# The last q/k group through a staging tile and small DMAs, with a new order of all operations

## The chip, the cores and the metric

The kernel runs on one core of a Trainium2 chip. The metric is the device time of that core in microseconds. Three runs of the kernel before took 193.17, 193.51 and 193.54 us; the median is 193.51. Texts below call the engines TensorE (PE in the profile; its weight loads PEld), VectorE (DVE), ScalarE (ACT), GpSimd (POOL) and SyncE (SP), which issues all DMAs here.

## The reference

The input x has 2048 rows of 448 numbers in bf16. Two layers are applied, each with a residual:

```python
h  = x + A(layernorm(x))          # qkv (448 x 1344), 16 heads of 28 channels,
                                  # 8 keys at distances 0, 2, .. 14 back, softmax, * wo
h2 = h + B(h):
  g  = gelu(layernorm(h) @ w1)    # 448 x 448
  hs = [g0 shifted +1, g1 shifted -1, g2 shifted +2, g3 shifted -2] @ w2   # four groups of 112 channels
  x1 = h + hs
  B  = x1 + gelu(layernorm(x1) @ w3) @ w4     # 448 x 1792, 1792 x 448
```

In the attention every query row reads only its own key and the seven keys 2, 4, .. 14 rows back. So a block of rows needs the last keys of the block before it.

## The kernel before, in words

**Stages.** The 2048 rows are handled in four steps t = 0..3 of 512 rows. For each the program has these phases; the digit behind a name is its t. N1 is the first normalization and A1 the transposes of x and the q and k channels (TensorE sums, copied out of PSUM, the banks where sums are made). V is the value channels. A2 is the products of queries and shifted keys on VectorE (four per step, c = 0..3, into `qk_r`), which TensorE adds up. S is the softmax, with the product `pb` (weights times reciprocal sum) and copies `pt` of its transposes. A3 builds band matrices on VectorE (`bd_r`, four per step), which TensorE multiplies with the values `vw`; copies `actT` bring the result out. O is the product with wo and the residual in `xin`. B1 is the next normalization with a DMA transpose, M the product with w1 and its gelu. Then the rows go through five units u = 0..4 of 2, 4, 4, 4 and 2 tiles of 128 rows: B2 (product with w2, residual), T (normalization and a DMA transpose), W3 (product with w3, gelu into `h3T`) and B3 (product with w4, last residual, and the store to the output). "A23" is phase A2 of step 3, "T0" phase T of unit 0, and so on.

**The last q/k group.** In A1 three pairs of groups hold 128 channels of q and of k each. The last 64 channels of q and of k stand in one pair of PSUM banks X and Y: X for the first 256 of the 512 rows, Y for the other 256, with q in partitions 0 to 63 and k in 64 to 127. q must go to `qT` (two halves of 64 partitions side by side), k to `kr`, which holds four runs of 64 keys on each of two halves of the partitions, and ahead of each run the PADK = 16 keys before it (the shared keys, or halo). Each step copies them with 8 operations (6 for t = 3): per bank one copy of q (64x256) and one of k (64x256), then a halo of 64x64, one of 64x48, and for t < 3 one of 64x16 into the next step's `kr` and one of 128x48 from `kk[t]` to `kk[t+1]`, the other keys' halo. These are 30 operations in all, of ScalarE but for one.

**What sets the order.** All operations are recorded with numbers by `S.add` and `S.group`. `arrange` puts them into the sequence that the list ORDER gives, which holds all numbers; every engine, and SyncE's queue of DMAs too, runs its own operations in that order. So an operation that waits holds back everything that stands behind it on its engine. Waits on semaphores follow from which data an operation reads and writes and from the buffers of the pools (`_Pool`): an operation that takes a buffer waits for all that used it last. The list OTHER names operations that go to their alternative engine: copies out of PSUM and norms have such an alternative, and the softmax product `pb` has GpSimd as its own (two of four are in OTHER). The strings NORM, STATS, POWER and the like choose engines of parts of the normalizations per step. All instructions are emitted at one line, L987, so in the profile names and shapes tell them apart, not lines. L982 loads a table of ScalarE's functions.

The copies in question:

```python
for h, b in enumerate((X, Y)):
    copy(qT[64 * h:64 * h + 64, 3, now:now + 256], b(lambda v: v[0:64, 0:256]))
    copy(kr[t][64 * h:64 * h + 64, :, PADK:], b(...v[64:128, 0:256]...), False)
copy(kr[t][64:128, :, 0:PADK], last(X, 0, 4), False)
copy(kr[t][0:64, 1:4, 0:PADK], last(Y, 0, 3), False)
```

The program's DMAs are loads (x in six pieces, then wqkv, wo, w1, w2, w3, w4), the copies of `vt` to `vw` (four per step, three for t = 0: vwa, vwb, vwc and vwp), one DMA transpose for each B1 and T, and the stores. The loads stand early in SyncE's order, the w4 loads among those of the attention.

Of the kernel before, what the change touches and what calls it, by code (L numbers as in the profile page):

```python
# [5 lines left out]
ACT = mybir.ActivationFunctionType  # L6
# [11 lines left out]
RESIDUAL = 'ttvv'  # L18
ORDER = """
# [30 lines left out]
"""  # L50
OTHER = """
104 127 196 197 199 402 408 411 519 525 528 582 583
# [79 lines left out]
class _Sched:  # L132
# [59 lines left out]
    def arrange(self, sequence, other=()):  # L192
# [4 lines left out]
        done = set()  # L197
        self.gorder = []
        for n, k in enumerate(sequence):
# [3 lines left out]
            op.deps |= op.sdeps  # L203
            for d in op.deps | op.odeps:
                if d not in done:
                    raise RuntimeError("operation %d (%s) stands before %d (%s)" % (k, op.tag, d.idx, d.tag))
# [68 lines left out]
def bass_sequential_preLN__sliding_local_dilated__mixer_s_mlp__prompt_kernel(  # L275
# [25 lines left out]
    A_W4 = A_W + 4 * (1344 + 128)  # L301
    A_QG = A_W4 + NF * 448
# [6 lines left out]
    with ExitStack() as es:  # L309
# [17 lines left out]
        st6 = sb("st6", [128, 8, 6], F32)  # L327
        mv = sb("mv", [128, 3, NTL, 2], F32)
# [20 lines left out]
        P_h3 = _Pool("h3", lambda k: h3T[:, k, :], NF + 2)  # L349
        P_st = _Pool("st", lambda k: st6[:, k, :], 8)  # L350
# [70 lines left out]
        def load_x(i, n):  # L421
            return dma("x%d" % i, xin[:, i:i + n, :], xv[:, i:i + n, :], 128 * n * D * 2)

        def load_rows(chan, dst, src, lo, n):

            for h in range(2):
                dma("%s%s" % (chan, "ab"[h]), dst[:, 2 * h:2 * h + 2, :], src[192 * h:192 * h + 256, lo:lo + n].rearrange("(c k) n -> k c n", k=128), 256 * n * 2)
# [21 lines left out]
        w4_v = B_w4.rearrange("(f k) n -> k f n", k=128)  # L449
        for f in range(0, NF, 7):  # L450
            dma("w4%d" % f, w4_s[:, f:f + 7, :], w4_v[:, f:f + 7, :], 128 * 7 * D * 2)
        for eng in ("sp", "pool", "act"):
            loads = [op for op in S.ops if op.tag == "load" and op.eng == eng]
            for a, b in zip(loads, loads[1:]):
                b.odeps.add(a)
# [164 lines left out]
        def setup_late(after):  # L620
# [18 lines left out]
            late("memset", ap=vw[0:PADK, 0, 0, :], constant=0.0)  # L639
            late("memset", ap=gT[:, :, 0:2], constant=0.0)  # L640
# [31 lines left out]
        def phase_A1(t):  # L672
# [356 lines left out]
```

## Time and profile before

| What | Value |
|---|---|
| median of three runs | 193.51 us (193.17 to 193.54) |
| the profiled execution: time, span | 193.18 us, 191.7 us |
| granted TensorE clock, mean | 0.999 |
| TensorE busy | 181.3 us, 95% of the span, 2482 matmuls |
| VectorE busy | 129.5 us, 68% |
| ScalarE busy | 132.9 us, 69% |
| GpSimd busy | 29.3 us, 15% |
| DMA, moved in all | 17.03 MB |
| chain that ended last | 66% TensorE, 21% ScalarE, 5% VectorE, 2% DMA |

The span is the time from the first to the last instruction of one profiled execution; the run's own time lies 1.5 us above it. Busy times are sums over an engine's instructions. The rows of the groups name what is written and what is read (`out<-in`), the shape, the count, the busy time, the mean of one in ns, and the idle time of the engine just ahead of them. The chain of waits goes back from the last instruction to what released each; in a timeline each row is a run of like instructions with start and duration.

### The profile page before, as it was taken

Reading aid. Unit: us, or ns where it says so; the run is one execution under the profiler, and the core shown is the slowest. Engines: PE = TensorE matmul, PEld = TensorE weight load, DVE = VectorE, ACT = ScalarE, POOL = GpSimd, SP = SyncE. Lnnn points to the kernel's source line nnn. Section 1 sums busy time; section 2 is a strip of 40 time slices with the busy share of each in tenths; the row PEclk is TensorE's granted clock in tenths of the full one; section 3 lists DMA queues with packets and bytes.
Section 4 is the critical chain, followed back from the end, with each engine's and each line's share of the span. In section 5 each row is a group of like instructions: output and inputs, shape, how many; then the busy total and the mean of one; then the engine's idle time right before and its main releaser. Section 6 shows DMA issues by size and latency. Waiting matters only on the chain.

```text
span 191.7 us, 5740 instructions
## 1 busy us (share of the span) xinstructions
PE 181.3 (95%) x2482; PEld 92.6 (48%) x2482; DVE 129.5 (68%) x229; ACT 132.9 (69%) x310; POOL 29.3 (15%) x63
## 2 busy tenths in 40 slices
PE   6999999999999868989999999999999999999994
PEld 2584533453444333347545444455444544555672
DVE  7799999999999999899876960036988022002203
ACT  4579999999999999999594998860148004821340
POOL 3240000000004000202076000022077600000000
PEclk9999999999999999999999999999999999999999
DMA  5999791004604179480805024006100812000111
GB/s 144 349 268 186 190 320 36 10 3 118 149 3 85 28 64 262 140 178 5 109 3 113 2 50 87 0 3 146 36 27 0 164 51 72 0 3 0 51 48 48
DMA packets 30272, 17.03 MB, mean 89 GB/s; under 512 B 18936, under 2 KB 29736, under 8 KB 30248
## 3 DMA queue, kind: packets, MB, share of 16 engines
q1 hardware_dynamic: 30248, 16.68, 36.7%
q8 instruction: 19, 0.31, 0.7%
q14 instruction: 5, 0.04, 0.1%
HBM read 8.04 MB, written 1.84 MB: 51 GB/s over the span
## 4 chain that ended last, share of the span: by engine, by line
PE 66%; ACT 21%; DVE 5%; DMA 2%; POOL 1%; issue 1%; SPq 1%; POOLq 0%; ACTq 0%
PE ps L987 66%; ACT arena L987 7%; ACT lntm L987 4%; ACT actT L987 2%; DMA vw<-vt 2%; ACT vt L987 2%; ACT L982 1%; DVE lntm L987 1%; DVE st L987 1%; SPq L987 1%; ACT xin L987 1%; ACT ls L987 1%; ACT L987 1%; DVE bd_r L987 1%; DVE actT L987 1%
## 5 line engine op out<-in xcount | busy, mean ns | idle before, releaser
L987 PE MATMUL ps<-actT,arena 64*128 64x256 bf16 (+1 forms) x756 | 68.8, 329 | 1.3 <-DVE arena L987 0.7
L987 ACT ACTIVATE h3T<-ps 128x512 bf16<-128x512 f32 (+1 forms) x70 | 30.3, 525 | 39.3 <-PE ps L987 39.2
L987 PEld LDWEIGHTS ps<-actT,arena 64*128 64x128 bf16 x756 | 35.5, 94 | 30.7 <-PE ps L987 2.1
L987 PE MATMUL ps<-arena,h3T 64*128 64x448 bf16 (+2 forms) x434 | 44.4, 344 | 0.0
L987 ACT ACTIVATE arena<-ps 128x512 bf16<-128x512 f32 (+10 forms) x86 | 40.1, 515 | 3.5 <-PE ps L987 2.8
L987 DVE SCALAR_TENSOR_TENSOR ost<-ps,mrs,arena 128x448 bf16<-128x448 f32 (+1 forms) x17 | 10.6, 652 | 36.4 <-PE ps L987 36.4
L987 DVE TENSOR_TENSOR qk_r<-arena 128x4096 bf16<-128x4096 bf16 (+1 forms) x16 | 32.0, 2017 | 0.7 <-PE ps L987 0.5
L987 PEld LDWEIGHTS ps<-arena,h3T 64*128 64x128 bf16 (+1 forms) x434 | 23.0, 94 | 18.7 <-issue 0.2
L987 POOL TENSOR_TENSOR arena<-arena,xin 128x448 f32<-128x448 f32 x16 | 17.2, 1091 | 45.3 <-DVE lntm L987 45.3
L987 DVE TENSOR_TENSOR bd_r<-arena,bmask 80x2048 bf16<-80x2048 bf16 x16 | 18.9, 1213 | 0.9 <-PE ps L987 0.7
L987 ACT ACTIVATE actT<-ps 128x512 bf16<-128x512 f32 (+2 forms) x21 | 14.6, 743 | 2.1 <-PE ps L987 2.1
L987 PE MATMUL ps<-wo_s,actT 64*128 64x448 bf16 x128 | 14.3, 351 | 0.6 <-DVE actT L987 0.4
L987 PE MATMUL ps<-actT,w_s 64*128 64x512 bf16 x112 | 13.3, 377 | 1.5 <-ACT rs_y L987 0.7
L987 PE MATMUL ps<-arena,actT 64*128 64x448 bf16 x112 | 12.4, 350 | 0.4 <-ACT vt L987 0.4
L987 PE MATMUL ps<-w_s,arena 64*128 64x448 bf16 x112 | 11.6, 350 | 0.9 <-ACT arena L987 0.7
L987 ACT ACTIVATE lntm<-xin,nm 128x448 bf16<-128x448 bf16 x16 | 10.5, 661 | 2.6 <-DVE nm L987 2.6
L987 DVE SCALAR_TENSOR_TENSOR arena<-xin,rs_y,ps 128x448 f32<-128x448 bf16 x16 | 10.3, 672 | 2.1 <-PE ps L987 2.0
L987 DVE TENSOR_SCALAR lntm<-arena,mv,rs_y 128x512 bf16<-128x512 f32 x14 | 10.2, 774 | 2.1 <-POOL rs_y L987 2.0
L987 POOL TENSOR_TENSOR pb<-ls,mx 128x512 bf16<-128x512 f32 x2 | 3.3, 1640 | 52.6 <-ACT mx L987 52.6
L987 DVE BATCH_NORM_STATS2 st<-xin 128x6 f32<-128x448 bf16 x16 | 9.4, 614 | 0.8 <-DMA xin<-in_A_x_dram 0.8
L987 PEld LDWEIGHTS ps<-actT,w_s 64*128 64x128 bf16 x112 | 5.2, 94 | 8.6 <-PE ps L987 1.7
L987 PEld LDWEIGHTS ps<-wo_s,actT 64*128 64x128 bf16 x128 | 5.6, 94 | 7.2 <-PE ps L987 1.4
(73 smaller groups left out, 161.9 us busy)
## 6 DMA issues: line engine op xcount, KB each, us to landing
arena<-in_B_w_dram SPq DMA_DIRECT2D x2, 896.0 KB, 6.7
out_dram<-ost SPq DMA_DIRECT2D x15, 112.0 KB, 1.8
arena<-in_B_w_dram SPq DMA_DIRECT2D x2, 784.0 KB, 5.7
vw<-vt SPq DMA_DIRECT2D x4, 320.0 KB, 4.3
vw<-vt SPq DMA_DIRECT2D x4, 256.0 KB, 4.3
arena<-in_A_wqkv_dram SPq DMA_DIRECT2D x2, 448.0 KB, 5.0
xin<-in_A_x_dram SPq DMA_DIRECT2D x2, 448.0 KB, 7.5
xin<-in_A_x_dram SPq DMA_DIRECT2D x3, 224.0 KB, 5.6
```

The costliest lines, as they stand in the source:

```text
L982: eng.preload_act_table_set("natural_log_exp_and_others")
L987: inst = getattr(eng, meth)(**kw)
```

## The change

Each bank of the last q/k group is copied whole (128x256) into a staging tile `stg`, of which there is one buffer. From there DMAs put the parts in place: two for q (`sq`), two for k (`sk`), and the halos by `kra`, `krb`, and for t < 3 `krc` and `kkc`. The 30 copies become 8 copies (of ScalarE, as the new OTHER has none of them) and 30 DMAs of 2 to 32 KB on SyncE.

Beside it:

- ORDER and OTHER are new. By the new OTHER, all four copies of A32, one more norm of B10 and one of T1 are on ScalarE (two of these copies and both norms were on VectorE); the other way go one copy 128x1024 of A12, one more copy of A10, one `vt` copy of V3 and one `pt` copy of S3. Of A33's four copies two are on VectorE as before, but not the same two.
- `pb` has no alternative any more: all four are on VectorE, where two were on GpSimd.
- NORM for unit 1 lets ScalarE do its norms, with VectorE as the alternative (three of four take it), which adds two small operations (`nm`, `nmr`) on VectorE.
- The tile for w4 lies over that of wqkv, and the w4 loads stand behind V3 (`load_w4`).
- Output staging has five buffers instead of three.
- The weight loads of wo, w1, w2 and w3 stand later in SyncE's order, among the small DMAs. krb3 stands right behind T0's DMA transpose, and two of V3's `vw` DMAs behind B12's.
- COPIED and ALONE are empty and false, and the code under them does nothing; more general slices in some sums change no instruction.

Operations go from 891 to 901, DMAs on SyncE from 71 to 101, ScalarE's operations from 272 to 251, VectorE's from 219 to 222, GpSimd's from 59 to 57. TensorE has the same matmuls.

```diff
-NORM = {'N0': 'vvvv', 'N1': 'avvv', 'B1': 'avvv', 'B2': 'avvvv'}
+NORM = {'N0': 'vvvv', 'N1': 'vvvv', 'B1': 'avvv', 'B2': 'aavvv'}
-NBD, NLN, NACT, NSM, NO = 3, 2, 4, 1, 3
+NBD, NLN, NACT, NSM, NO = 3, 2, 4, 1, 5
+HALO = 'dddd'
+STAGE = 'dddd'
 ORDER = """
...
 OTHER = """
-104 127 196 197 199 402 408 411 519 525 528 582 583
+99 104 196 199 355 502 529 533 539 590 591 652 653 654
...
-    A_W4 = A_W + 4 * (1344 + 128)
-    A_QG = A_W4 + NF * 448
+    A_W4 = A_W
+    A_QG = A_W4 + max(NF * 448, 4 * (1344 + 128))
...
+        P_sg = _Pool("sg", lambda k: stg[:, k, :, :], 1)
...
             duo(half(X, 0, True), half(Y, 64, False), ((0, 256),))
-            for h, b in enumerate((X, Y)):
-                copy(qT[64 * h:64 * h + 64, 3, now:now + 256], b(lambda v: v[0:64, 0:256]))
-                copy(kr[t][64 * h:64 * h + 64, :, PADK:], b(lambda v: v[64:128, 0:256].rearrange("p (j n) -> p j n", j=4)), False)
-            copy(kr[t][64:128, :, 0:PADK], last(X, 0, 4), False)
-            copy(kr[t][0:64, 1:4, 0:PADK], last(Y, 0, 3), False)
-            if t + 1 < NST:
-                copy(kr[t + 1][0:64, 0:1, 0:PADK], last(Y, 3, 1), False)
-                copy(kk[t + 1][:, :, 0:PADK], kk[t][:, :, 512:KVW])
+            if STAGE[t] == "d":
+                stage = _Tile(P_sg)
+                for h, b in enumerate((X, Y)):
+                    copy(stage(lambda v, h=h: v[:, h, :]), b(lambda v: v[:, 0:256]))
+                for h in range(2):
+                    dma("sq%d%d" % (t, h), qT[64 * h:64 * h + 64, 3, now:now + 256], stage(lambda v, h=h: v[0:64, h, :]), 64 * 512)
+                    dma("sk%d%d" % (t, h), kr[t][64 * h:64 * h + 64, :, PADK:], stage(lambda v, h=h: v[64:128, h, :].rearrange("p (j n) -> p j n", j=4)), 64 * 512)
...
+            if HALO[t] == "d":
+                if STAGE[t] == "d":
+                    end = lambda h, lo, n: stage(lambda v: v[64:128, h, :].rearrange("p (j n) -> p j n", j=4)[:, lo:lo + n, 64 - PADK:])
...
+                dma("kra%d" % t, kr[t][64:128, :, 0:PADK], end(0, 0, 4), 64 * 4 * PADK * 2)
+                dma("krb%d" % t, kr[t][0:64, 1:4, 0:PADK], end(1, 0, 3), 64 * 3 * PADK * 2)
+                if t + 1 < NST:
+                    dma("krc%d" % t, kr[t + 1][0:64, 0:1, 0:PADK], end(1, 3, 1), 64 * PADK * 2)
+                    dma("kkc%d" % t, kk[t + 1][:, :, 0:PADK], kk[t][:, :, 512:KVW], 128 * 3 * PADK * 2)
...
-            S.add("dve", "tensor_tensor", alts=[("pool", [("tensor_tensor", mult)])], **mult)
+            dve("tensor_tensor", **mult)
...
+        def load_w4():
+            last = S.ops[-1]
+            w4_v = B_w4.rearrange("(f k) n -> k f n", k=128)
+            for f in range(0, NF, 7):
+                dma("w4%d" % f, w4_s[:, f:f + 7, :], w4_v[:, f:f + 7, :], 128 * 7 * D * 2).odeps.add(last)
```

More of the change, by code (lines that the diff above doesn't have):

```diff
@@ L203, in arrange @@
             op.deps |= op.sdeps
+            if not ALONE:
+                pass
+            elif op.insts[0][0] == "dma_start_transpose":
+                op.deps.update(turned + moved)
+                turned, moved = [op], []
+            elif op.is_dma and not callable(op.chan):
+                op.deps.update(turned)
+                moved.append(op)
             for d in op.deps | op.odeps:
@@ L327, in bass_sequential_preLN__sliding_local_dilated__mixer_s_mlp__prompt_kernel @@
         st6 = sb("st6", [128, 8, 6], F32)
+        stg = sb("stg", [128, 1, 2, 256], BF16)
+        gM = sb("gM", [128, max(1, len(COPIED)), QGW], BF16) if COPIED else None
         mv = sb("mv", [128, 3, NTL, 2], F32)
@@ L448, in bass_sequential_preLN__sliding_local_dilated__mixer_s_mlp__prompt_kernel @@
         load_rows("w3", w3_s, B_w3, 0, F)
[L449 to L455, printed above, removed]
+        loads = [op for op in S.ops if op.is_dma]
+        for a, b in zip(loads, loads[1:]):
+            b.odeps.add(a)
         TOP, BOT = slice(0, 64), slice(64, 128)
@@ L639, in setup_late @@
             late("memset", ap=vw[0:PADK, 0, 0, :], constant=0.0)
+            if COPIED:
+                late("memset", ap=gM[64:128, :, 0:2], constant=0.0)
+                late("memset", ap=gM[64:128, :, 2 + SEQ:4 + SEQ], constant=0.0)
             late("memset", ap=gT[:, :, 0:2], constant=0.0)
@@ new lines, in phase_A1 @@
+            if HALO[t] == "d":
+                if STAGE[t] == "d":
+                    end = lambda h, lo, n: stage(lambda v: v[64:128, h, :].rearrange("p (j n) -> p j n", j=4)[:, lo:lo + n, 64 - PADK:])
+                else:
+                    end = lambda h, lo, n: kr[t][64 * h:64 * h + 64, lo:lo + n, 64:]
+                dma("kra%d" % t, kr[t][64:128, :, 0:PADK], end(0, 0, 4), 64 * 4 * PADK * 2)
[3 more added lines that the diff above has]
+                    dma("kkc%d" % t, kk[t + 1][:, :, 0:PADK], kk[t][:, :, 512:KVW], 128 * 3 * PADK * 2)
+            else:
+                copy(kr[t][64:128, :, 0:PADK], last(X, 0, 4), False)
+                copy(kr[t][0:64, 1:4, 0:PADK], last(Y, 0, 3), False)
+                if t + 1 < NST:
+                    copy(kr[t + 1][0:64, 0:1, 0:PADK], last(Y, 3, 1), False)
+                    copy(kk[t + 1][:, :, 0:PADK], kk[t][:, :, 512:KVW])
@@ L847, in evict @@
                         lo, m, early = MOVED[g]
-                        at = 2 + t * 512 - early
+                        now = 2 + t * 512
+                        at = now - early
                         skip = max(0, -at)
-                        act(gT[lo:lo + m, g, at + skip:at + 512], b(lambda v: v[lo:lo + m, skip:]), ACT.Gelu_apprx_tanh)
+                        to = gM if g in COPIED else gT
+                        if g in COPIED:
+                            dma("gm%d%d" % (t, g), gM[lo:lo + m, g, at + skip:at + 512], gT[lo:lo + m, g, now + skip:now + 512], m * 1024)
+                            rest = slice(64, lo) if lo > 64 else slice(lo + m, 128)
+                            dma("gn%d%d" % (t, g), gM[rest, g, now:now + 512], gT[rest, g, now:now + 512], (64 - m) * 1024)
+                        else:
+                            act(gT[lo:lo + m, g, at + skip:at + 512], b(lambda v: v[lo:lo + m, skip:]), ACT.Gelu_apprx_tanh)
                         if t == NST - 1:
-                            dve("memset", ap=gT[lo:lo + m, g, at + 512:at + 512 + early], constant=0.0)
-                return sums(lambda lo, n: b(halves(lambda v: v)), lambda c, part: w1_s[part, c, g * 128:(g + 1) * 128],
-                            lambda c, part, lo, n: rows(a, c, 0, 4, part), upper), evict
+                            dve("memset", ap=to[lo:lo + m, g, at + 512:at + 512 + early], constant=0.0)
+                return sums(lambda lo, n: b(halves(lambda v: v[:, lo:lo + n], n // 128)), lambda c, part: w1_s[part, c, g * 128:(g + 1) * 128],
+                            lambda c, part, lo, n: rows(a, c, lo // 128, n // 128, part), upper), evict
             for g in (0, 2):
@@ L874, in side @@
                     part = (TOP, BOT)[h]
-                    return [(gT[part, c, 2 + i * 128 + SHIFT[c, h]:130 + i * 128 + SHIFT[c, h]], (lambda lo, m, c=c: w2_s[part, c, lo:lo + m])) for c in range(n)]
+                    return [((gM if h and c in COPIED else gT)[part, c, 2 + i * 128 + SHIFT[c, h]:130 + i * 128 + SHIFT[c, h]], (lambda lo, m, c=c: w2_s[part, c, lo:lo + m])) for c in range(n)]
                 def out():
@@ L910, in group @@
                 b = _Tile(P_bank)
-                return sums(lambda lo, m: b(halves(lambda v: v[:, 0:128 * n], n)), lambda c, part: w3_s[part, c, f * 128:(f + 1) * 128],
-                            lambda c, part, lo, m: rows(a, c, 0, n, part), upper), \
+                return sums(lambda lo, m: b(halves(lambda v: v[:, lo:lo + m], m // 128)), lambda c, part: w3_s[part, c, f * 128:(f + 1) * 128],
+                            lambda c, part, lo, m: rows(a, c, lo // 128, m // 128, part), upper), \
                     lambda: act(h3[u][f](lambda v: v[:, 0:128 * n]), b(lambda v: v[:, 0:128 * n]), ACT.Gelu_apprx_tanh)
```

22 lines of the change are left out of this document (16 added, 6 removed), and 60 rows, old and new, of the table ORDER.

## The prediction

> **What bounds the kernel now.** I read the busy time by stage first, because the page's 95% for TensorE is a mean over stages with different limits. The columns are the stretch in us, its length, and busy time and count of each engine.
>
> ```profile
> 60.00:76.00 16.00, 12.69 (x250) 5.86 (x248) 15.76 (x25) 15.60 (x36) 2.20 (x1) 1.00 0.63 116
> 76.00:88.00 12.00, 11.02 (x132) 5.11 (x130) 11.13 (x26) 11.71 (x26) 2.56 (x4) 1.00 0.55 148
> 88.00:104.00 16.00, 15.53 (x300) 8.67 (x302) 12.50 (x25) 12.72 (x29) 5.97 (x7) 1.00 0.35 53
> 104.00:188.00 84.00, 84.00 (x871) 43.92 (x868) 32.05 (x71) 39.30 (x81) 13.30 (x15) 1.00 0.19 45
> ```
>
> From 104 to 188 us TensorE (first count) is busy all the time and the other two less than half of it, so nothing done to VectorE or ScalarE there can shorten it. From 60 to 88 us VectorE and ScalarE are both full, and TensorE is idle for 3.31 + 0.98 = 4.3 us; from 88 to 104 us for another 0.47 us. The granted clock is 1.00 throughout. So the kernel ends earlier only if TensorE idles less ahead of about 100 us: there are 4.8 us to be had in these stretches, and lighter work on one of two full engines brings them only if the other gets no heavier.
>
> The chain of waits says where the last stretch without a gap begins:
>
> ```profile
> 100.41 87.81 PE ps L987 x907
> ```
>
> Hence I look for the event that releases this stretch. It is an `actT` copy on VectorE, which the two timelines about that moment show (start, duration, engine, operation; in brackets the idle time ahead and its releaser):
>
> ```profile
> 94.58 1.22 DVE L987 TENSOR_TENSOR bd_r<-arena,bmask 80x2048 bf16<-80x2048 bf16 x1 [0.70 <-PE ps L987]
> 95.72 0.68 DVE L987 CAST actT<-ps 128x512 bf16<-128x512 f32 x1
> 96.33 0.23 DVE L987 BATCH_NORM_AGGREGATE mv<-st 128x2 f32<-128x6 f32 x2
> 96.59 0.17 DVE L987 TENSOR_SCALAR rs_x<-mv 128x4 f32<-128x4 f32 x1
> 97.90 1.86 DVE L987 TENSOR_SCALAR lntm<-arena,mv,rs_y 128x512 bf16<-128x512 f32 x2 [1.14 <-POOL rs_y L987]
> 99.68 0.68 DVE L987 CAST actT<-ps 128x512 bf16<-128x512 f32 x1
> ```
> ```profile
> 98.14 0.42 PE L987 MATMUL ps<-bd_r,vw 80*32 80x64 bf16 x32
> 98.49 1.50 PE L987 MATMUL ps<-arena,h3T 64*128 64x448 bf16 x14
> 100.41 0.93 PE L987 MATMUL ps<-wo_s,actT 64*128 64x448 bf16 x8 [0.43 <-DVE actT L987]
> ```
>
> The last band product of attention (94.58) ends at 95.80; the TensorE batch that reads it starts 2.34 us later, so that wait had room. The copy that O3 (·wo of the last 512 rows) needs stands behind two of T1's norms, which waited 1.14 us for GpSimd's power: TensorE lost 0.43 us there.
>
> **The change on ScalarE.** All 30 small copies of the last q/k group leave the engines; eight copies 128x256 from PSUM come instead. The groups by shape (busy us, mean ns):
>
> ```profile
> L987 ACT ACTIVATE h3T<-ps 128x256 bf16<-128x256 f32 x28 | 8.6, 406 | 11.1 <-PE ps L987 11.0
> ...
> L987 ACT ACTIVATE actT<-ps 128x512 bf16<-128x512 f32 x12 | 6.8, 615 | 2.1 <-PE ps L987 2.1
> L987 ACT ACTIVATE actT<-ps 128x1024 bf16<-128x1024 bf16 x6 | 6.2, 1077 | 0.0
> L987 ACT ACTIVATE arena<-ps 64x256 bf16<-64x256 f32 x15 | 5.6, 376 | 2.3 <-PE ps L987 2.1
> ...
> L987 ACT ACTIVATE arena<-ps 64x64 bf16<-64x64 f32 x4 | 0.9, 216 | 0.1
> L987 ACT ACTIVATE arena<-arena 128x48 bf16<-128x48 bf16 x3 | 0.8, 268 | 0.0
> L987 ACT ACTIVATION_READ_ACCUMULATOR xin<-ps 128x1 f32 x4 | 0.8, 201 | 0.0
> L987 ACT ACTIVATE lntm<-xin,nmr,rs_y 128x512 bf16<-128x512 bf16 x1 | 0.8, 803 | 0.0
> ```
>
> Out: 5.6 + 0.9 + 0.8 = 7.3 us, and four copies 64x48 and three 64x16, each at no more than the 0.216 of the 64x64 row, 1.5 at most. In: eight at 0.376 (64x256) to 0.406 (128x256, with gelu), about 3.1. Net 5 to 5.7 us lighter. The new list of operations that use their alternative engine swaps others: four copies leave ScalarE (A12's transpose copy at 1.077; another transpose copy, one of V3 and one of S3, each at most 0.615: 2.9 us) and two copies of A32 and one norm each of B10 and T1 come (2 x 0.615 + 2 x 0.803 = 2.8 us): nothing. ScalarE thus has some 5 us less to do, all of it before 88 us.
>
> **The change on VectorE**, the other full engine, is what I put the sum on. I count the work that the new order and the new list place ahead of the last band product (the 94.58 row), in prices of these rows and of the timeline:
>
> ```profile
> L987 DVE TENSOR_TENSOR qk_r<-arena 128x4096 bf16<-128x4096 bf16 x12 | 27.3, 2283 | 0.2 <-ACT arena L987 0.2
> ...
> L987 DVE TENSOR_SCALAR lntm<-arena,mv,rs_y 128x512 bf16<-128x512 f32 x14 | 10.2, 774 | 2.1 <-POOL rs_y L987 2.0
> ...
> L987 DVE SCALAR_TENSOR_TENSOR xin<-ps,xin 128x448 bf16<-128x448 f32 x8 | 4.7, 622 | 1.8 <-PE ps L987 1.5
> ...
> L987 DVE TENSOR_TENSOR pb<-ls,mx 128x512 bf16<-128x512 f32 x2 | 1.4, 683 | 0.0
> ...
> L987 DVE COPY actT<-ps 128x512 bf16<-128x512 bf16 x1 | 0.4, 425 | 0.2 <-PE ps L987 0.2
> ```
>
> In: three of T1's norms at 0.774 = 2.32, with three small operations ahead of them (0.17 each, 0.5) and two aggregates (0.23 + about 0.1); the softmax products of t = 2 and 3, which lose GpSimd as an alternative, 2 x 0.683 = 1.37; the copies of V3 and S3 and one more of A33's, 3 x 0.68 = 2.04; A12's copy of twice the 0.425 row, 0.85, and A10's, 0.43. Together 7.8 us. Out: two A32 copies 1.36, and a half of the q copy, one of B10's norms and a small operation, about 0.4 + 0.4 + 0.17; together 2.3. Net 5.5 us later. Two idle times change: the 0.70 us ahead of 94.58 goes, as TensorE is then the earlier; and T1's norms now wait ahead of the band product for GpSimd's power (the 1.14 of the row, less one 0.17 operation put into it, about 0.9). The band product ends at 95.80 + 5.5 - 0.7 + 0.9 = 101.5 us.
>
> TensorE's own work ahead of the batch that reads it also grows: two halves of B3 (14 matmuls each) and one of O3 (8) stand ahead of it now. 36 matmuls at 84.00 us / 871 = 0.096 us are 3.5 us, so TensorE comes to it at 98.14 + 3.5 = 101.6. Both meet: what ScalarE gains is eaten by VectorE's queue, and the 2.34 us of room at this place are used up. What is left is the end of this knot: O3 no longer waits for a copy that stands behind norms and a power (its other copy is on ScalarE), so the 0.43 us of TensorE and the 0.1 or so of it that the thin batch before it loses are saved: **0.5 us**. After that TensorE has the same 84 us of work to do; M3 and W32, whose inputs come through later DMA transposes, come out even in the same count (0 to 0.4 us of room), and B2's and the last unit's work is the same.
>
> **The added DMAs and waits.** 30 small DMAs go onto SyncE's queue, which carries 71 before. The nearest rows are the small transfers of `vw`, the transposes and a store (last number: us from issue to landing), and the times that SyncE takes to issue (a transpose, then ns min/median/max for `vw`):
>
> ```profile
> vw<-vt SPq DMA_DIRECT2D x4, 48.0 KB, 3.6
> actT<-lntm SPq DMA_TRANSPOSE x9, 4.3
> out_dram<-ost SPq DMA_DIRECT2D x2, 56.0 KB, 1.6
> ...
> vw<-vt SPq DMA_DIRECT2D x3, 16.0 KB, 4.8
> ```
> ```profile
> 80.72 1.26 SPq L987 DMA_TRANSPOSE actT<-lntm  x1
> ```
> ```profile
> L987 SPq DMA_DIRECT2D vw<-vt x15: 567/667/1526, 19.3 to 82.7; - x15
> ```
>
> A DMA in place of a copy thus costs its reader nothing while its turn on SyncE (0.67 us for each ahead of it) and 1.6 to 4.8 us of landing lie beside other work. Four places are near that. *The one staging buffer*: ScalarE's first staging copy of the next 512 rows waits until the last small DMA has landed. At t = 1 that is nine issues, 6.0 + 1.6 to 4.8 = 7.6 to 10.8 us, with an x load among them, against some 15 ScalarE operations at about 0.62, 9.5 us; at t = 2 ten issues, 8.3 to 11.5, against 18 or so, 11; at t = 3 three issues behind the V1 copies, 3.6 to 6.8, against 11, 7. A stall of 0 to 1.3 us would stand ahead of ScalarE's `vt` copies and q/k copies and be paid out of its 5 us; I take none. *wo* is now loaded four issues behind the V1 copies, and O0 reads it after much the same 7 us: none by the 1.6 row, 0.5 by the 4.8 row, and TensorE has idle time there. *V3's two vw transfers* stand behind B12's transpose: they land at most 2 x 0.67 + 4.8 - 4.3 = 1.8 us after it, and the 28 matmuls of M2, which the transpose releases, take at least 28 x 0.096 = 2.7 us (the mean is worked out above): none. *krb3* is the tight one: VectorE's fourth product of A23 waits for it, and it stands on SyncE right behind T0's transpose. From T0's last norm to that product VectorE has one product (2.283), two residuals of O2 (1.24), a small operation (0.17) and a `vt` copy (0.68): 4.4 us of cover. The transpose's issue (1.26) and a landing of 1.6 to 4.8 make 2.9 to 6.1. The stall is 0 to 1.7 us; behind it is queued the rest of attention's VectorE work, and for it wait TensorE's sums and all of S3. I take none, because three small DMAs in a burst, as in the 16 KB row, are not what stands there: a lone one is nearer to the 56 KB store. 1.7 is kept for the range; none of these can be a gain, since a reader at its earliest just does not wait.
>
> The overlay of w4 on the qkv weights puts two loads behind V3 on SyncE and costs nothing as long as they land ahead of B30, 10 us later; five output buffers instead of three touch only the last stretch, where TensorE never waits.
>
> The Trainium skill, page "DMA: Bandwidth & Descriptors", section "Measured", says that transfers under 64 KB are dominated by their descriptors, and its section "Anatomy of one DMA", for transfers issued from GpSimd, gives a fixed 2.0 us plus the size by 436 GB/s: 2.04 us for 16 KB, an estimate by that page. The 4.8 us row above is over twice that, and the measurement decides; by the page's figure the landing at 3.3 us would lie inside the cover.
>
> **The rivals.** *ScalarE's relief passes through* (faster). If TensorE is held by ScalarE's copies rather than VectorE's products between 60 and 88 us, the 4.3 us idle there shrink, and T1's norms run undisturbed. For it: ScalarE is as full as VectorE there, and two staging copies free a bank pair sooner than eight. Against: VectorE is full too, and heavier by 1.4 us in total (0.43 + 0.85 + 0.68 + 0.68 + 1.37 + 0.3 in, 0.38 + 0.4 + 1.36 + 0.77 out). If the 0.9 us wait is filled and the two waits about T1 (0.43 and a half us beside it) go with some 0.3 of bank waits: about -1.7, 191.8 us, or 191.5 with 0.3 more of bank waits.
>
> *krb3 lands late* (slower). One mechanism at one place: krb3 behind the transpose. It decides as soon as krb3 lands later than 4.4 - 1.26 = 3.1 us after its issue. For it: the 4.8 and 3.6 rows are above that. Against: the 1.6 row. The band product has no room left by the sum above, so the whole stall reaches TensorE: 1.7 less the 0.5, so +1.2, 194.7 us; with a further wait behind the W3 loads issued just before, 195.0. The Trainium skill, same page, section "Queues, rings and completion order", says that on each DMA engine descriptors are consumed in ring order; by that rule this rival would hold, and the rows so far show only 16 KB transfers that land slowly in a burst, which does not tell it.
>
> *Nothing comes of it* (the same). VectorE's 1.4 us and the power wait take the last 0.5 as well: 193.5 us, up to 193.9 if the M3 and W32 transposes use up their 0.4.
>
> **How the numbers follow.** The profiled execution took 193.18 us for a span of 191.7; less 0.5 it would be 192.7. The median of the three runs is 0.33 above it, so against the median the same step gives 193.51 - 0.5 = 193.0. A measurement of this kernel can tell about 0.2%, 0.39 us, from no change. Chances: forecast 0.45, with a range of its own from 192.2 (the pair of idle times worth 0.8 more) to 193.9; ScalarE's relief 0.2; krb3 0.2; nothing 0.15. The range reaches from 191.5 to 195.0: it takes in both ends of the fast rival and of the slow one, and leaves out what is beyond. Faster: three fifths of the forecast's 0.45 (below 193.1) and all of 0.2, 0.47. Slower: the 0.2, a third of the last 0.15 and 0.05 of the forecast, 0.30. The same: the rest, 0.23.
>
> **What would show it right or wrong.** Right: the 128x256 copies at 0.38 to 0.41 us, eight of them; no VectorE idle time ahead of the fourth product of A23; the last band product ending at 101 to 102 us, and O3's start without an idle TensorE; TensorE's busy sum within 0.3 us of before, its idle ahead of 104 us smaller by about 0.5. Wrong to the fast side: TensorE idle from 60 to 88 us falls from 4.3 to under 3. Wrong to the slow side: the wait table shows a `kr` DMA as the releaser of a `qk_r` product by a microsecond or more, or TensorE waits at M3 or W32 behind a transpose.

## The result, and the profile after

The kernel after takes **198.36 us** (median of four runs, 197.62 to 200.09) against 193.52 before: a ratio of 1.026, 95% interval 1.0219 to 1.0301. It is slower by 4.8 us, and outside the range of the prediction. The profiled execution (200.09 us, span 198.3) is the longest of the four; it holds a second stretch of halved TensorE clock, which the others lack by their mean clock (0.991 against 0.982).

Busy time by stage, in the columns of the prediction:

```profile
60.00:76.00 16.00, 13.39 (x278) 5.91 (x274) 15.73 (x26) 15.51 (x37) 0.00 (x0) 0.97 0.56 116
76.00:88.00 12.00, 11.69 (x114) 4.44 (x112) 10.53 (x22) 10.09 (x21) 0.00 (x0) 0.89 0.49 159
88.00:104.00 16.00, 15.51 (x200) 8.37 (x196) 14.54 (x30) 14.48 (x34) 4.50 (x5) 1.00 0.78 183
104.00:120.00 16.00, 14.53 (x258) 7.17 (x258) 14.62 (x29) 12.08 (x26) 7.04 (x5) 1.00 0.18 36
```

TensorE still idles for 16.00 - 14.53 = 1.47 us between 104 and 120 us, and its granted clock (third column from the end) is not full throughout. The chain of waits (start, duration, engine, name) shows where the last stretch without a gap begins and the first place where time was lost ahead of it:

```profile
27.46 0.65 SPq L1037
28.11 0.04 issue
28.16 5.04 DMA arena<-stg
33.20 0.03 ACTq L1035
33.23 0.04 issue
33.27 0.10 ACT stg L1037
...
34.48 12.56 PE ps L1037 x240
...
109.02 86.80 PE ps L1037 x924
```

Here and below `...` stands for rows left out. The last stretch begins at 109.02 us instead of 100.41 and is 1.0 us shorter, so everything was lost ahead of it. ScalarE's staging copy for t = 2 waits for a DMA out of the one staging buffer, and that DMA stands at the end of a row of SyncE issues (seven more such rows of 0.4 to 0.7 us lie ahead of the first one here). The issues about it, with KB and us to landing:

```profile
vw<-vt SPq DMA_DIRECT2D x1, 320.0 KB, 5.6
vw<-vt SPq DMA_DIRECT2D x1, 256.0 KB, 4.8
arena<-stg SPq DMA_DIRECT2D x1, 6.0 KB, 2.4
arena<-stg SPq DMA_DIRECT2D x1, 2.0 KB, 5.0
```

krc1, 2 KB, takes 5.0 us where krb1 of 6 KB, issued just ahead of the 320 KB `vw` transfer, takes 2.4. The waits of ScalarE and TensorE that follow, and the stretches about them:

```profile
ACT stg L1037 <- DMA arena<-stg: 2.5, 1, 2.5
PE ps L1037 <- ACT stg L1037: 2.2, 1, 2.2
```
```profile
31.00:33.70 2.70, 0.54 (x6) 0.10 (x2) 1.77 (x2) 0.43 (x2) 0.00 (x0) 1.00 0.53 106
33.70:34.60 0.90, 0.74 (x10) 0.25 (x12) 0.23 (x1) 0.90 (x3) 0.00 (x0) 0.77 0.00 0
34.60:38.00 3.40, 3.40 (x20) 1.25 (x19) 3.40 (x5) 2.61 (x9) 0.00 (x0) 0.56 0.17 17
38.00:44.00 6.00, 6.00 (x136) 2.82 (x132) 4.08 (x6) 5.46 (x10) 0.00 (x0) 1.00 0.57 134
```

TensorE idles for 2.2 us and then has 0.56 of its clock for 3.4 us: 0.44 x 3.4 = 1.5 us of work lost after the wait has ended. The second such stretch of this execution stands elsewhere (TensorE alone; the clock is again third from the end):

```profile
74.00:75.00 1.00, 0.42 (x34) 1.00 1.37 206
75.00:76.00 1.00, 1.00 (x8) 0.57 0.66 197
76.00:77.00 1.00, 0.94 (x8) 0.50 0.98 369
77.00:78.00 1.00, 1.00 (x8) 0.50 1.06 380
78.00:79.00 1.00, 1.00 (x8) 0.72 1.04 418
```
```profile
74.42 0.42 PE L1037 MATMUL ps<-bd_r,vw 80*32 80x64 bf16 x32 [0.63 <-DVE bd_r L1037]
```

The longest idle time of TensorE in the 7 us ahead of it is 0.63 us. So a stretch of halved clock does not need a wait as long as the one for the staging buffer, and where the single one of the other three executions stood is not on record.

The second place is about the last band product. The same rows as in the prediction, VectorE first, then GpSimd:

```profile
101.65 5.34 DVE L1037 TENSOR_TENSOR bd_r<-arena,bmask 80x2048 bf16<-80x2048 bf16 x3
106.92 0.68 DVE L1037 CAST actT<-ps 128x512 bf16<-128x512 f32 x1
107.52 1.45 DVE L1037 TENSOR_TENSOR bd_r<-arena,bmask 80x2048 bf16<-80x2048 bf16 x1
```
```profile
100.69 9.17 POOL L1037 TENSOR_TENSOR arena<-arena,xin 128x448 f32<-128x448 f32 x5 [1.82 <-DVE lntm L1037]
```

Three band products take 5.34 us, 1.78 each, where one took 1.22; five of GpSimd's adds take 9.17 us, 1.83 each. Before, T1's adds ran from 97.98 us on, after the last band product had ended at 95.80:

```profile
97.98 1.04 POOL L987 TENSOR_TENSOR arena<-arena,xin 128x448 f32<-128x448 f32 x1
```

Now the order lets the two run side by side. The last band product ends at 108.97 us; the forecast was 101.5. The busy time up to that moment, before and after:

```profile
0.00:95.80 95.80, 88.65 (x1502) 44.43 (x1504) 90.95 (x146) 86.63 (x219) 10.02 (x42) 1.00 0.56 132
```
```profile
0.00:108.97 108.97, 97.10 (x1558) 48.75 (x1558) 98.32 (x155) 88.87 (x204) 14.89 (x45) 0.97 0.53 127
```

VectorE (third engine) works 98.32 - 90.95 = 7.4 us more ahead of it and idles 108.97 - 98.32 = 10.65 us instead of 4.85.

The third place is the first A31 product on TensorE:

```profile
57.16 0.42 PE L1037 MATMUL ps<-bd_r,vw 80*32 80x64 bf16 x32 [1.58 <-DVE bd_r L1037]
```
```profile
52.90 1.52 SPq L1037 DMA_DIRECT2D vw<-vt  x2
```
```profile
vw<-vt SPq DMA_DIRECT2D x1, 48.0 KB, 3.3
```

The profile names VectorE's `bd_r` as the releaser, but its band products had all three ended by 56.8 us, the first at 54.5:

```profile
53.29 3.48 DVE L1037 TENSOR_TENSOR bd_r<-arena,bmask 80x2048 bf16<-80x2048 bf16 x3
```

The second of the two issues from 52.90 is V1's 48 KB transfer at 53.80; with 3.3 us to landing it is there at 57.1, which is when the product starts. Where the engine named has long been done, one looks for a DMA.

The prediction had named signs. Two came as forecast: the eight staging copies take 0.379 us each, and the fourth product of A23 has no idle time ahead of it. Three did not: the last band product ends at 108.97 us, O3 still waits 0.73 us for a copy, and TensorE's busy time is 183.9 us instead of 181.3, since work at a lower clock takes longer. The sign for the fast side was met although the kernel is slower: TensorE's idle time from 60 to 88 us is 2.61 + 0.31 = 2.9 us, under 3. A fixed stretch of time holds other work once the kernel is late, so it is no sign by itself. And no sign looked at the staging buffer or at V0's and V1's transfers.

### The profile page after: what moved, and what is told of

Read it like the earlier page. It is cut to its first block, busy times and chain, and to the rows that moved or that the text cites. A ratio compares the mean times of both kernels' runs of the same rounds, so it can differ in the third digit from the quotient of the medians.

```text
span 198.3 us, 5769 instructions
## 1 busy us (share of the span) xinstructions
PE 183.9 (93%) x2482; PEld 94.1 (47%) x2482; DVE 131.8 (66%) x232; ACT 129.2 (65%) x289; POOL 29.5 (15%) x61
## 4 chain that ended last, share of the span: by engine, by line
PE 55%; DVE 24%; DMA 8%; ACT 5%; SPq 5%; issue 1%; POOL 1%; ACTq 0%; DVEq 0%
PE ps L1037 55%; DVE bd_r L1037 7%; DMA xin<-in_A_x_dram 5%; DVE qk_r L1037 5%; SPq L1037 5%; DVE lntm L1037 3%; DMA arena<-stg 3%; DVE st L1037 2%; DVE arena L1037 2%; ACT arena L1037 1%; ACT stg L1037 1%; DVE pb L1037 1%; DVE mx L1037 1%; ACT lntm L1037 1%; ACT actT L1037 1%
## 5 line engine op out<-in xcount | busy, mean ns | idle before, releaser
L1037 PE MATMUL ps<-actT,arena 64*128 64x512 bf16 (+1 forms) x756 | 70.3, 331 | 0.8 <-DVE actT L1037 0.5
L1037 PEld LDWEIGHTS ps<-actT,arena 64*128 64x128 bf16 x756 | 36.2, 94 | 29.9 <-PE ps L1037 1.6
L1037 ACT ACTIVATE arena<-ps 128x512 bf16<-128x512 f32 (+7 forms) x59 | 33.0, 597 | 3.9 <-PE ps L1037 3.5
L1037 DVE SCALAR_TENSOR_TENSOR ost<-ps,mrs,arena 128x448 bf16<-128x448 f32 (+1 forms) x17 | 10.7, 653 | 32.7 <-PE ps L1037 27.5
L1037 POOL TENSOR_TENSOR arena<-arena,xin 128x448 f32<-128x448 f32 x16 | 20.8, 1322 | 36.0 <-DVE lntm L1037 36.0
L1037 DVE TENSOR_TENSOR bd_r<-arena,bmask 80x2048 bf16<-80x2048 bf16 x16 | 21.0, 1344 | 1.1 <-PE ps L1037 0.9
L1037 POOL TENSOR_TENSOR rs_y<-rs_x,mhalf 128x4 f32<-128x4 f32 (+1 forms) x3 | 2.8, 917 | 94.1 <-DVE nm L1037 86.2
L1037 PE MATMUL ps<-w_s,arena 64*128 64x448 bf16 x112 | 13.6, 374 | 0.2 <-issue 0.2
L1037 PE MATMUL ps<-qk_r,zc 128*32 128x512 bf16 x112 | 8.1, 383 | 2.3 <-ACT stg L1037 2.2
L1037 PE MATMUL ps<-bd_r,vw 80*32 80x64 bf16 x512 | 6.6, 194 | 3.4 <-DVE bd_r L1037 2.5
L1037 DVE TENSOR_SCALAR lntm<-arena,mv,rs_y 128x512 bf16<-128x512 f32 x13 | 6.7, 540 | 4.2 <-ACT rs_y L1037 3.0
```

Of the source, the lines that this page charges most:

```text
L1037: inst = getattr(eng, meth)(**kw)
```

## The experiments

Theories: **S**, the single staging buffer. **Q**, the order of SyncE's queue, in which `vw` transfers and small DMAs hold each other up. **P**, GpSimd's adds beside the band products. **D**, VectorE's longer queue, the term on which the forecast was built. All times are medians; each ratio is to runs of the kernel before on the same chip. Those medians lie between 193.52 and 193.97 us from chip to chip, so small differences between experiments are taken from the ratios, which are good to some 0.3% (0.6 us) each. All four runs of the kernel after have a mean clock of 0.991 or less; most kernels below have runs at 1.00 too, which can be a part of a gain.

**Two staging buffers**

```diff
-        stg = sb("stg", [128, 1, 2, 256], BF16)
+        stg = sb("stg", [128, 2, 2, 256], BF16)
-        P_sg = _Pool("sg", lambda k: stg[:, k, :, :], 1)
+        P_sg = _Pool("sg", lambda k: stg[:, k, :, :], 2)
```

> The kernel after with two staging buffers instead of one, nothing else. Theory S (the single buffer: ScalarE's staging copy of t = 2 waits 2.49 us for krc1's landing, TensorE then idles 2.16 us and runs at half clock for some 3.4 us, which costs 1.7 more): that wait and that clock dip go, 3.9 us less at that place, so 194.3 to 195.5 us. Theory P (GpSimd's adds slow the band products of t = 3) or D (VectorE's queue is simply 5.5 us heavier): 197.5 to 198.4, as the lost time is lost later anyway.

Measured: 196.47 us (195.79 to 198.40), ratio 1.016 (1.012 to 1.0201). The wait for the buffer is gone, but only 1.9 of the expected 3 to 4 us. The next wait is a few operations on: a `vt` copy on ScalarE stands still for 1.89 us.

```profile
33.70 0.98 ACT L1037 ACTIVATE vt<-ps 128x448 bf16<-128x448 f32 x2 [1.89 <-DMA vw<-vt]
```

It overwrites what V0's vw transfers have yet to read, the very transfers that stand behind the small DMAs. S alone is too narrow.

**krc1 ahead of the vw transfer**, on SyncE only:

```diff
-  krb1 vwb0 krc1 vwa0
+  krb1 krc1 vwb0 vwa0
```

> The kernel after with one staging buffer, but krc1 (2 KB) issued ahead of the 320 KB vw transfer behind which it landed after 5.04 us. Theory S with the queue as the cause of the late landing: krc1 lands about 2 us after its issue, at about 29.5 us instead of 33.2, and the staging copy waits less than 0.5 us; 194.3 to 196. If the landing was late for another reason: 198 as before.

Measured: 196.81 us (195.75 to 198.12), ratio 1.0168 (1.0129 to 1.0206). The staging copy still waits 0.9 us, and the `vt` copy 0.9. One place in the queue brings 1.6 us with one buffer. But only a part of what was expected came: the DMA that the copy waits for still lands late.

```profile
arena<-stg SPq DMA_DIRECT2D x1, 6.0 KB, 2.4
arena<-stg SPq DMA_DIRECT2D x1, 2.0 KB, 4.1
```

krc1, now issued some 0.7 us ahead of the 320 KB transfer, takes 4.1 us instead of 5.0, not the 2 that were expected. So what stood ahead of it is not the whole cause of the late landing; a large transfer issued right behind it is there in both kernels. With both of V0's large transfers far ahead (the three moves below) krc1 takes 2.6 us.

**GpSimd's adds later**

```diff
-  S.add("pool", "tensor_tensor", out=xb[i], in0=xb[i], in1=xin[:, i, :], op=ALU.add).block = True
+  S.add("pool", "tensor_tensor", out=xb[i], in0=xb[i], in1=xin[:, i, :], op=ALU.add,
+        after=[S.ops[534]] if u < 2 else []).block = True      # 534: the last band product
```

> The kernel after, but GpSimd's adds of units 0 and 1 (128x448, f32) wait for the last band product of t = 3. Theory P: band products back from 2.05 to 1.21 us, adds from 2.01 to 1.03, 1.9 us less ahead of the last long stretch: 196.4 to 197. Theory S or D alone: within 0.4 us of 198.4.

In ORDER the first of these adds moves behind the last band product with it. Measured: 196.13 us (195.28 to 196.91), ratio 1.0128 (1.0099 to 1.0156): 2.2 us less than the kernel after.

```profile
98.80 3.49 DVE L1037 TENSOR_TENSOR bd_r<-arena,bmask 80x2048 bf16<-80x2048 bf16 x3
```
```profile
104.30 5.00 POOL L1037 TENSOR_TENSOR arena<-arena,xin 128x448 f32<-128x448 f32 x5 [8.28 <-DVE bd_r L1037]
```

Three products take 3.49 instead of 5.34 us, five adds 5.00 instead of 9.17: P holds.

**Both**, two buffers and the later adds:

> Two staging buffers and the adds held back. S and P both true and independent: 192.5 to 193.8, that is no slower than before. D (VectorE's heavier queue): 195 or more remains.

Measured: 196.16 us (195.24 to 197.27), ratio 1.0134 (1.01 to 1.0168). They do not add up: the `vt` copy waits 1.7 us, and TensorE's first A31 product still waits, 1.36 us, for V1's 48 KB transfer. The time lies where D expected it; the next kernels tell D from the queue.

**The new order with the old copies**: the staging and its 30 DMAs are undone and the order is kept.

```diff
-HALO = 'dddd'
-STAGE = 'dddd'
+HALO = 'cccc'
+STAGE = 'cccc'
```

> The order and engine choice of the kernel after, but with the copies of before in place of the staging and its 30 DMAs (all on ScalarE, at the places of the staging copies). ScalarE gets its 5 us back, SyncE's queue loses 30 issues. Theory S (the staging's waits cost the time): no staging wait, GpSimd's contention remains: 194.5 to 196. Theory D (the new order loads VectorE by 5.3 us ahead of the last band product and that alone costs): 196 to 198, and more if ScalarE now is the late one.

Measured: 199.06 us (198.94 to 200.29), ratio 1.0273 (1.0241 to 1.0304). No wait for a `vw` transfer or a staging buffer is left, and it is no faster. ScalarE is the late one (a burst of eight small copies takes 2.74 us ahead of a `vt` copy), and the adds run beside the band products (9.16 us for five). Since ScalarE's 5 us are back, this kernel alone does not tell S from D; it shows that the new order is slow without the staging too.

**vw transfers ahead**, beside two buffers and later adds. V0's two big vw transfers go ahead of the second 512 rows' small DMAs:

```diff
-  kra0 sq10 sq11 vwc0 sk10 kra1 vwp1 sk11 krb1 vwb0 krc1 vwa0
+  kra0 vwb0 vwa0 sq10 sq11 vwc0 sk10 kra1 vwp1 sk11 krb1 krc1
```

> Two staging buffers, GpSimd's adds held back, and V0's two vw transfers (256 and 320 KB) issued ahead of the small DMAs of the second 512 rows. With two buffers ScalarE waited 1.73 us for one of them before a vt copy. If SyncE's queue is what is left of the loss: that wait goes, 194.6 to 195.4 us. If VectorE's queue is (theory D): 195.8 to 196.4 as without.

Measured: 193.99 us (193.14 to 195.51, 12 runs), ratio 1.0016 (0.9989 to 1.0042). Two places on a queue whose transfers are the same bring 2.2 us, and the kernel is not measurably slower than before. VectorE's work is unchanged, so D does not carry the loss. One more execution of this kernel was taken, as a base:

> The kernel e137 once more, for a profile at full clock, as a base for the two kernels with it: 193.1 to 194.5.

It took 195.19 us at a mean clock of 0.991; the runs of this kernel at 1.00 lie at 193.1 to 194.5.

**Three moves on SyncE's queue alone.** The kernel after with nothing else changed: V0's two transfers as above, and V1's 48 KB transfer ahead of the last small DMAs of t = 2.

```diff
-  kra0 sq10 ...                    vwb1 sk20 sk21 wo ... vwc1
+  kra0 vwb0 vwa0 sq10 ...          vwb1 vwc1 sk20 sk21 wo ...
```

> The kernel after with nothing changed but three places on SyncE's queue: V0's two big vw transfers ahead of the second 512 rows' small DMAs, V1's 48 KB one ahead of the third's. One staging buffer, GpSimd's adds beside the band products as they were. Theory Q (the order of SyncE's queue is the main cause): 194.2 to 195.4, that is 3 to 4 us of the 4.8; theory S (the one buffer): 196 or more, since it still waits.

Measured: 195.24 us (194.61 to 196.07, 9 runs), ratio 1.0092 (1.0062 to 1.0121). Of the 4.8 us, 3.1 go by the order of one queue. It is not the clock alone: the three runs at a mean clock of 0.991 take 195.94 to 196.07 us, the three of the kernel after at 0.991 197.62 to 198.38. The staging copy still waits 1.41 us, as S says.

**All of it**: two buffers, later adds, and the three moves.

> The kernel with two staging buffers, adds held back and V0's two vw transfers ahead (193.99 us), plus one move: V1's 48 KB vw transfer ahead of the last small DMAs of t = 2, so that TensorE's first A31 product does not wait 2.13 us for it. If that idling reaches the end: 192.0 to 193.0. If VectorE's queue ahead of the last band product holds the end anyway: 193.6 to 194.2.

Measured: **192.57 us** (192.21 to 193.58, 10 runs), ratio 0.9935 (0.9906 to 0.9963): faster than the kernel before, by 1.2 us, and by the medians 5.8 us faster than the kernel after. Its rows at the places shown:

```profile
51.95 0.42 PE L1037 MATMUL ps<-bd_r,vw 80*32 80x64 bf16 x32
```
```profile
95.46 3.49 DVE L1037 TENSOR_TENSOR bd_r<-arena,bmask 80x2048 bf16<-80x2048 bf16 x3
99.21 0.69 DVE L1037 CAST actT<-ps 128x512 bf16<-128x512 f32 x1 [0.26 <-PE ps L1037]
99.82 1.21 DVE L1037 TENSOR_TENSOR bd_r<-arena,bmask 80x2048 bf16<-80x2048 bf16 x1
```
```profile
0.00:101.03 101.03, 93.26 (x1522) 47.98 (x1524) 95.75 (x155) 88.40 (x203) 6.57 (x40) 1.00 0.58 137
```
```profile
98.19 0.53 issue
98.72 90.03 PE ps L1037 x1042
188.75 0.02 issue
188.78 0.45 DVE ost L1037
```

The first A31 product has no wait ahead of it, the last band product ends at 101.03, and TensorE runs without a gap from 98.72 on. That is 2.3 us ahead of the end of the last band product, so here it is no longer the event that the last stretch waits for; TensorE comes to the batch that reads it half a us after it:

```profile
101.53 0.70 PE L1037 MATMUL ps<-bd_r,vw 80*32 80x64 bf16 x64
```

**The two halves of the rest.** Between the three moves alone (195.24) and the best version (192.57) lie the buffer and the adds. With the mended queue, one of them at a time (the edits as above):

> The kernel after with SyncE's three moves and GpSimd's adds held back; one staging buffer. If the adds beside the band products are most of the 2.7 us between the three moves alone (195.24) and the best version (192.57): 193.0 to 193.6. If the one buffer is: 194.6 to 195.2.

> The kernel after with SyncE's three moves and two staging buffers; the adds as in the kernel after. If the one buffer is most of the 2.7 us: 193.0 to 193.6. If the adds are: 194.4 to 195.2. If both halves add up: about 194 in both kernels.

Measured: 194.45 us with the adds later (193.16 to 195.68, 12 runs; ratio 1.0028, 0.9998 to 1.0058) and 193.68 with two buffers (193.09 to 195.00, 12 runs; ratio 1.0014, 0.9984 to 1.0045). By the ratios (1.0092, 1.0028, 1.0014, 0.9935) the buffer brings 0.78% or 1.5 us and the adds on top of it 0.79% or 1.5; the other way about the adds bring 1.2 and the buffer 1.8, each good to some 0.8 us. Neither is most of it.

**Less on VectorE**: the three moves, buffer and later adds, and beside them a softmax product moved into T1's wait for GpSimd and two of T1's norms given to ScalarE.

```diff
-  (VectorE) nm nmr norm pb norm norm          (652 653 in OTHER)
+  (VectorE) nm pb nmr norm                    (652 653 not in OTHER)
```

> e137 with V1's 48 KB vw transfer ahead of the second 512 rows' last small DMAs (it landed at 53.41 us as the last of a burst, and TensorE's first A31 product started at 53.50 after 2.13 us of idling), and less on VectorE ahead of the last band product: T1's wait for GpSimd is filled with a softmax product, two of T1's norms are on ScalarE. If SyncE's order is the cause of that idling: it goes, 192.0 to 192.8. If VectorE's queue holds the time in addition: 191.4 to 192.2. If neither: 194.

Measured: 193.79 us (193.54 to 194.67, 12 runs), ratio 1.001 (0.9984 to 1.0035): 1.2 us slower than without. This is the time expected for "neither", but the move of V1's transfer alone (192.57) had already shown that its idling counts; what is lost here comes from VectorE's new list. VectorE has less to do and waits more:

```profile
93.08 0.69 DVE L1037 TENSOR_TENSOR pb<-ls,mx 128x512 bf16<-128x512 f32 x1 [1.80 <-ACT mx L1037]
...
96.62 3.49 DVE L1037 TENSOR_TENSOR bd_r<-arena,bmask 80x2048 bf16<-80x2048 bf16 x3 [1.28 <-ACT arena L1037]
```

The product moved ahead stands waiting for ScalarE's exponent, and the band products for a copy that now lies behind the norms.

**Staging in the order of before**, with four buffers, the small DMAs right behind the staging copies, and w4 laid over wqkv to make room:

```diff
-  (SyncE) wqkv x x wo ... w2 ... vwa0
+  (SyncE) sk00 sk01 kra0 krb0 krc0 sq00 sq01 wqkv x x wo ... w2 ... vwa0
```

> The order and engine choice of the kernel before, with staging (four buffers, no reuse), the small DMAs right behind the staging copies, and w4 laid over wqkv to make room. VectorE as before but for 0.4 us less, ScalarE 5 us lighter. Theory Q (30 more issues cost only where a vw transfer or a staging reuse stands behind them): 192.3 to 193.7. Theory W (the small DMAs delay vw transfers in any order): above 194.5, with TensorE waiting for vw.

Measured: 215.08 us (214.49 to 215.50), ratio 1.1102 (1.1059 to 1.1145). The four buffers leave nothing for S, and VectorE's list is the old one, so none of D. The largest wait is this one:

```profile
20.70 0.63 DVE L1016 BATCH_NORM_STATS2 st<-xin 128x6 f32<-128x448 bf16 x1 [9.47 <-DMA xin<-in_A_x_dram]
```

The next x loads stand behind seven small DMAs that wait for the staging copies, the first issued at 10.9 us; the loads follow at 16.9, where before they were issued at 5.7 and 6.6. W is seen as well: ScalarE's `vt` copies wait 7.0 us and TensorE 1.9 us for `vw` transfers, and the mean clock is 0.944.

With the small DMAs of t = 0 behind the loads up to w2, krc1 behind V0's vw transfer, and V1's big transfers ahead of t = 2's:

> Staging in the order of before, as in the 215 us kernel, but the small DMAs of t = 0 stand behind the x and weight loads up to w2, krc1 behind V0's vw transfer, and V1's two big vw transfers ahead of the small DMAs of t = 2. Theory Q (the cost lies in what waits behind the small DMAs on SyncE's queue): the 8.5 us that TensorE waited for an x load and most of the vw waits go, 194 to 199 us. If staging is bad in itself: above 205.

Measured: 198.77 us (195.93 to 200.58), ratio 1.0198 (1.013 to 1.0266). The placing of the same DMAs is worth 16 us. VectorE still waits for them:

```profile
36.11 1.22 DVE L1016 TENSOR_TENSOR qk_r<-arena 128x2048 bf16<-128x2048 bf16 x1 [3.46 <-DMA arena<-stg]
```

The small DMAs of t = 1 have too little time here between the staging copy and the fourth product: the six of them issued from 26.13 to 29.73 us took 6.0 to 8.6 us, behind a weight load of 896 KB that was issued at 25.50 and took 9.0, and ahead of vw transfers of 320 and 256 KB. So the large load ahead of them may be a cause beside their own place, which was not tested. Whether another placing, or the old order with one buffer, would make staging pay was not measured.

## Why the prediction was wrong, point by point

**The bound** was read rightly: what decides is when TensorE's last stretch without a gap begins. In the kernel after that hangs on the last band product of t = 3 (108.97, then 109.02), as it does in the versions with the adds beside the products (105.10, then 105.14 with krc1 ahead; 107.59, then 107.64 with the old copies). With the adds held back it begins ahead of that product's end (98.72 and 101.03 in the best version).

**ScalarE's part** was right. The eight staging copies take 0.379 us each, at the lower end of 0.376 to 0.406, and the relief is real: the new order with the old copies takes 199.06 us, with staging, mended queue and two buffers 193.68, both with the adds where they were.

**VectorE's sum** was right as far as it went. It said 5.5 us more ahead of the last band product and its end at 101.5 us. In the best version VectorE has 95.75 - 90.95 = 4.8 us more there, and the product ends at 101.03; TensorE comes to the batch that reads it at 101.53, where the forecast said 101.6. That kernel takes 192.57 us, 1.2 less than the kernel before beside it, where the forecast was 0.5 less. It has three corrections that the predicted kernel lacks, so its nearness to the forecast of 193.0 does not make the forecast right, and the 0.7 us more are not accounted for. What the kernel after has beyond its forecast is 2.1 us of band products slowed by GpSimd (5.34 + 1.45 us for four, 3.49 + 1.21 without) and idle time.

**The step that failed is "the added DMAs and waits", where the cost was taken as none.** It fails in three ways.

- *The one staging buffer.* For t = 2 the landing was put at 8.3 to 11.5 us behind the staging copies and ScalarE's cover at 11. Measured, the last DMA landed at 33.20, which is 10.7 us after the copies of t = 1 had ended at 22.47: near the upper end, beside transfers of 320 and 256 KB. ScalarE's operations between them took only 8.3 us, so the cover is the term that was mis-sized. A stall of 0 to 1.3 us, said to be paid out of ScalarE's 5 us, was 2.49 us and reached TensorE, which idled for 2.2.
- *The vw transfers behind the small DMAs.* The step looked at what the small DMAs wait for and at V3's `vw` transfers, but not at V0's and V1's, which the same queue carries. V0's two big ones landed at 33.0 and 33.7 us; ahead of the small DMAs they land at 25.5 and 26.8. They held a `vt` copy, and V1's 48 KB one held a TensorE product. The three moves give back 3.1 us.
- *The clock.* No stall was priced beyond its own length. In the profiled execution the one of 2.2 us was followed by a halved clock that took 1.5 us more. That the wait caused it was not shown: the other stretch of the same execution stands behind gaps of at most 0.63 us.

**What was not seen at all** is P. The new order moves GpSimd's adds and VectorE's band products to the same place, and each was taken at the duration that it has alone. The trace of before showed the adds at 1.03 us from 97.98 on, after the band products; that they would meet could have been read off the new order. With the queue and the buffer mended and the adds left as they are, the kernel takes 193.68 us (ratio 1.0014, 0.9984 to 1.0045), about the time of before; the adds alone, mended first, bring 2.2 us. The shares depend on what is mended first.

**The slow rival** was one small DMA, krb3 behind T0's transpose. It did not hold: krb3 landed 2.0 us after its issue, and the fourth A23 product had no wait. Its mechanism, a small DMA that lands late because of a larger one ahead, was in the main the right one, at the wrong place: krc1 took 5.0 us behind 320 KB. The Trainium skill, page "DMA: Bandwidth & Descriptors", section "Queues, rings and completion order", says that descriptors are consumed in ring order on each DMA engine; krc1 and krb1 of the kernel after agree with it (5.0 us behind the large transfer, 2.4 ahead of it), but by that order alone krc1 issued ahead of the 320 KB transfer would not have taken 4.1; why it did stays open.

**The fast rival** (ScalarE's relief passes through) was at 191.8 us, and the forecast at 193.0; the best version, 192.57, lies between them, but it is another kernel than the one forecast. The terms of that rival as they are written, 0.9 + 0.43 + 0.5 + 0.3, come to 2.1 us and not to 1.7.

## What to carry to other kernels

Small DMAs instead of copies can cost little in themselves, but they take turns on an in-order queue: for each one, list what stands behind it there and who waits for that, and for each transfer that it overtakes, the buffer that it was to set free. An engine made lighter comes sooner to its next wait, so the cover of a wait has to be counted with the new loads. When an order is searched anew, look which operations of VectorE and GpSimd now run side by side, and do not price them alone. And take a wait that has gone as a gain only when the end of the kernel has moved: the next wait often stands right behind it.

## What the runs showed of the hardware

- In the kernel after, the small transfers out of the staging tile (2, 6, 8 and 32 KB) land 1.8 to 2.2 us after their issue (medians by size), those of 12 KB 3.0. The 2 KB krc1 took 5.0 us when a 320 KB transfer was issued 0.7 us ahead of it on the same queue, 4.1 when that was issued 0.7 us behind it, and 2.6 with neither. The Trainium skill's fixed 2.0 us, which it gives for transfers issued from GpSimd (page "DMA: Bandwidth & Descriptors", section "Anatomy of one DMA"), agrees with the medians; the 4.8 us that the prediction took as the upper price of a small transfer was a median of three, and the one looked at was issued 0.6 us behind a weight load of 784 KB.
- VectorE's band product (two bf16 inputs from SBUF, 1.21 us alone) and GpSimd's f32 add (1.00 us alone, 5.00 us for five) slow each other to 1.78 and 1.83 us on average, and to 2.05 and 2.01 where they overlap throughout. The Trainium skill, page "SBUF — State Buffer", section "SBUF: two separate sides", has them share a pair of ports under an exclusive lock, not a split bandwidth; in that case, as an estimate from these times, a pair that alternates would take about the sum of both, 2.2 us, which is near.
- After an idle time of about 2.2 us TensorE had 0.56 of its clock for 3.4 us, and 0.57 from 75 to 79 us, behind gaps of at most 0.63 us. Such dips come in some executions of a kernel and not in others: with two buffers alone, three runs at a mean clock of 0.991 took 197.0 to 198.4 us and three at 1.00 took 195.8 to 196.0.
